# A convolution and expert kernel of one core: the mask of tiny weights leaves the start, and seven squares, two taps and dummy products move

## The chip, the cores and the metric

The kernel runs on one core of a Trainium2 chip. The metric is the device time of one launch in microseconds (us), the median of several runs. In the profile PE is TensorE, DVE is VectorE, ACT is ScalarE, POOL is GpSimd and SP is SyncE, which here only issues transfers.

## The reference

Two stages follow each other. The first is a causal convolution of seven taps whose weights are a softmax for each position and head. The second is a two-layer network whose activation is a ratio of polynomials.

```python
w = softmax(weight_gen, axis=-1)                   # (4, 4096, 8 heads, 7 taps)
out = np.einsum('bshk,bskhg->bshg', w, x_unf)      # x_unf: 7 shifted copies of x (4, 4096, 192)
x = out.reshape(16384, 192)
h = x @ w_in                                       # w_in (192, 2048), float64
P = a[0] + a[1] * h + a[2] * h2 + a[3] * h3
Q = 1.0 + np.abs(b[0]) * np.abs(h) + np.abs(b[1]) * h2
out = (P / (Q + 1e-06)) @ w_out                    # w_out (2048, 192), float64
```

`weight_gen` and `b` are drawn eight times wider than the rest. The ratio |b0| / (2 sqrt |b1|) is 0.774 for the inputs used here.

## The kernel before

**Tiling.** The 16,384 tokens are cut into 32 chunks of 512, and the 2,048 hidden columns into 8 pairs of 128-column blocks. One chunk with one pair is a slot, so there are 256 slots. Slot n begins a new chunk when n is a multiple of 8.

**A slot.** `m1` (L708) makes the hidden block by 18 products of 512 columns: single-pass products of the high and low parts of data and weights. Then ACT takes |h| (`v1`, L742) and a shifted square (`z1`, L746). DVE forms v(v + rb) from |h| (`d1`, L750), ACT takes its logarithm (`ln`, L759) and an exponential of the negative (`ex`, L762), which is the reciprocal of the denominator. DVE forms the cubic (`w1`, L754) and the ratio (`gg`, L766). `m2` (L721) multiplies by `wo` in two halves of 16 products, `fore` and `aft`. Between the halves stands a `relay`, an empty instruction of SP (L783). The hidden block lies in PSUM in one of three buffers named `h`, so `m1` of slot n + 3 waits for `gg` of slot n. In the start one of the three is taken by `TMP`, the scratch of the weight work.

**Weights.** `w_in` and `w_out` are float64. They are loaded in 14 units: A0 to A3 and B0, B1 for `w_in`, W0 to W7 for `w_out`. `unit` turns each into float32 by hand: ACT reads the low words (`ua2`, L401) and takes the size of the high words (`ua1`, L397), DVE does four steps (`ub1` L406, `ub2` L411, `ub3` L416, `ub4` L421). The step `ub4` multiplies by (size >= TINY), so that a weight below 2^-126 becomes zero. For A and B units the value is then split in a high part (`uh`, ACT, L449) and a low part (`uw`, DVE, L452). Slot n waits for unit W of number n, for A of number n // 2 and for B of number n // 4. Four buffers named `raw` take the loads.

**Chunks.** `chunk` prepares the data: softmax of the tap weights, seven taps, transposition on PE, split by ACT and DVE (L650 to L662), and copies between partitions by transfers (`xd`, `xs`, L672 and L678). All chunks but the first have their taps on POOL (L560, L572, L578). In the first chunk (`early`) DVE does all seven taps (L560) and PE adds them up by products with an identity (`fold`, L596). WARM products with the identity stand before that on PE (L274).

**Order.** All of this is a list of operations with an engine, a duration, a priority key and dependences. `arrange` turns it into one fixed order for each engine by playing it through with the durations written in the list. `OFF`, `KEY`, `PITCH` and `PATIENCE` steer it. An operation with `lock` (here `d1`) is held back in that play while POOL is busy. After the launch's work the kernel reads the flag `slow`, which `judge` (POOL) sets from `a` and `b`; if it is set, a second, plain version runs.

Of the kernel before, what the change touches and what calls it, by code (L numbers as in the profile page):

```python
# [8 lines left out]
FP32 = mybir.dt.float32  # L9
# [35 lines left out]
PITCH = 4.8729  # L45
OFF = {
    "g": 12.72, "ex": 3.33, "ln": 5.25, "v": 13.04, "z": 5.74, "d": 7.0, "w1": 3.82, "m2": 3.16,
    "aft": 4.99, "step": 2.35, "cast": -1.03, "rest": -13.5, "dup": 13.03, "lead": 14.38,
    "w": 45.09, "wW": 10.62, "one": -7.23, "ahead": 52.98, "ul": -53.2,
}  # L50
KEY = {
    "B0": -29.4, "A0": -28.0, "W0": 32.8, "A1": 30.0, "W1": 12.93, "W2": 43.45, "W3": 10.63,
    "B1": 41.25, "A2": 50.17, "W4": 51.8, "W5": 52.8, "A3": 52.8, "W6": 63.24, "W7": 76.41,
# [4 lines left out]
START = 25.2  # L58

# [31 lines left out]
PATIENCE = 0.302  # L91


def arrange(ops, place):
# [48 lines left out]
    while len(order) < len(ops):  # L143
# [34 lines left out]
        if o.land is not None:  # L178
            pipe = max(pipe, o.end + 1.3) + o.land / RATE
            o.land = pipe + 0.4 - s  # L180
# [12 lines left out]

LAP = {"ACT": 0.09, "DVE": 0.08, "POOL": 0.05}
LOCK = 2.59
RATE = 230.0
LOOSE = ("h", "av", "pv", "g", "mag", "rnd", "t1", "w")
# [3 lines left out]
def kernel(  # L201
# [18 lines left out]
    ab = const.tile([P, 6], FP32, name="ab")  # L220
    mg = const.tile([P, 6], FP32, name="mg")
    cf = const.tile([P, 15], FP32, name="cf")
# [9 lines left out]
    tt = const.tile([P, 2], FP32, name="tt")  # L232
    steep = rt[:, 0:1]
    slow = const.tile([P, 1], I32, name="slow")
# [44 lines left out]
    o_mg = op("ACT", 0.2, -90.0, lambda: nc.scalar.activation(  # L279
        out=mg, in_=ab, func=ACTF.Abs), [o_ab])  # L280
# [25 lines left out]
    o_sg = op("POOL", 0.4, -70.0, sg_, [o_mg])  # L306
# [61 lines left out]
    def unit(u):  # L368
# [46 lines left out]
        def ub3():  # L415
            nc.vector.tensor_tensor(t["w"], t["w"], t["rnd"], op=ALU.add)  # L416
# [560 lines left out]
```

## Time and profile before

| what | value |
|---|---|
| median of 3 runs | 1304.03 us (1303.81 to 1304.39) |
| profiled execution | 1304.49 us, span 1302.7 us |
| PE, DVE, ACT, POOL busy | 1266.2, 1178.8, 1135.5, 863.3 us |
| mean granted clock of PE | 0.987 |

The profiled execution's time has 1.8 us around the span, from the first to the last instruction. A granted clock of 1.0 is 2.4 GHz, one of 0.5 is 1.2 GHz. Busy shares are averages over a start and a long even part and have to be read for each.

### The profile page before, as it was taken

The page shows a single profiled execution, that of the slowest core. Times are in us where ns is not written, and L with a number is a line of the kernel's source. Part 1 is how long each engine was busy: PE and PEld are TensorE (multiplying, and loading weights), DVE is VectorE, ACT ScalarE, POOL GpSimd, SP SyncE. Part 2 cuts the span into 40 slices and gives each one's busy share as a digit, 9 for nine tenths or more (in the row PEclk, how much of TensorE's full clock was granted, in tenths as well). Part 3 has the DMA queues.
Part 4 walks back from the last instruction along what each step waited for, and adds up shares of the span by engine and source line. Part 5 has one row for each costly group of instructions (what it writes and reads, how often), then busy time and mean ns, then how long its engine had stood idle before and what let it go on. Part 6 is the DMA issues. An engine that isn't in the chain of part 4 may idle for free.

```text
span 1302.7 us, 30683 instructions
## 1 busy us (share of the span) xinstructions
PE 1266.2 (97%) x13082; PEld 1154.6 (89%) x13082; DVE 1178.8 (90%) x979; ACT 1135.5 (87%) x1162; POOL 863.3 (66%) x578
## 2 busy tenths in 40 slices
PE   7679999999999999999999999999999999999998
PEld 5568989999999999999999999999899999999997
DVE  7989889999999999999999999999999999999884
ACT  3768989889998988989988989898899998898995
POOL 3945797787666688666678766668866667876200
PEclk8789999999999999999999999999999999999999
DMA  7422212222122122223122122212222212222100
GB/s 182 121 76 79 50 62 55 74 79 80 50 76 62 53 80 79 49 79 77 41 74 80 49 76 80 59 55 80 49 80 76 79 41 74 49 75 80 46 13 15
DMA packets 46291, 89.07 MB, mean 68 GB/s; under 512 B 5426, under 2 KB 27976, under 8 KB 46148
## 3 DMA queue, kind: packets, MB, share of 16 engines
q1 hardware_dynamic: 45860, 87.05, 24.3%
q8 instruction: 104, 1.70, 0.6%
q14 instruction: 39, 0.32, 0.1%
q10 hardware_dynamic: 288, 0.00, 0.0%
HBM read 41.40 MB, written 12.58 MB: 41 GB/s over the span
## 4 chain that ended last, share of the span: by engine, by line
PE 88%; DVE 3%; POOL 3%; ACT 2%; SPq 1%; issue 1%; DMA 1%; DVEq 0%; ACTq 0%; POOLq 0%
PE acc L721 49%; PE h L708 38%; PE h L640 1%; POOL pr L560 1%; POOL at L572 1%; SPq L672 1%; DMA x<-in_x_dram 1%; DVE g L766 0%; ACT av L742 0%; PE h L643 0%; SPq L678 0%; DVE av L750 0%; DVE h L411 0%; DVE xm L662 0%; ACT av L759 0%
## 5 line engine op out<-in xcount | busy, mean ns | idle before, releaser
L721 PE MATMUL acc<-wo,g 64*128 64x192 f32 x8192 | 722.1, 324 | 8.5 <-DVE g L766 5.0
L721 PEld LDWEIGHTS acc<-wo,g 64*128 64x128 f32 x8192 | 682.5, 187 | 37.3 <-SPq L783 8.1
L750 DVE SCALAR_TENSOR_TENSOR av<-av,cf 128x1024 f32<-128x1024 f32 x256 | 464.3, 1814 | 57.7 <-ACT av L742 57.5
L560 POOL TENSOR_TENSOR pr<-x,wn 128x768 f32<-128x768 f32 x186 | 364.8, 1961 | 0.1
L766 DVE SCALAR_TENSOR_TENSOR g<-h,ab,av 128x1024 f32<-128x1024 f32 x256 | 327.2, 1278 | 37.2 <-ACT av L762 33.2
L742 ACT ACTIVATE av<-h 128x1024 f32<-128x1024 f32 x256 | 260.2, 1016 | 82.4 <-PE h L708 78.5
L754 DVE SCALAR_TENSOR_TENSOR h<-pv,cf,h 128x1024 f32<-128x1024 f32 x256 | 326.7, 1276 | 0.8 <-ACT pv L746 0.8
L759 ACT ACTIVATE av<-av,c 128x1024 f32<-128x1024 f32 x256 | 293.0, 1145 | 37.1 <-DVE av L750 37.1
L572 POOL TENSOR_TENSOR at<-at,pr 128x768 f32<-128x768 f32 x155 | 312.5, 2016 | 12.2
L746 ACT ACTIVATE pv<-h,cf,rt 128x1024 f32<-128x1024 f32 x256 | 306.9, 1199 | 0.0
L762 ACT ACTIVATE av<-av 128x1024 f32<-128x1024 f32 x256 | 270.2, 1056 | 3.3
L708 PE MATMUL h<-xm,wh 64*128 64x512 f32 x1024 | 241.6, 461 | 15.4 <-DVE g L766 13.7
L708 PE MATMUL h<-xs,wh 64*128 64x512 f32 x1024 | 208.7, 394 | 1.7 <-DMA xs<-xm 1.7
L708 PE MATMUL h<-xd,wh 64*128 64x512 f32 x1024 | 206.8, 393 | 0.0
L523 POOL TENSOR_SCALAR mx<-mx,cf 128x32 f32<-128x32 f32 x31 | 9.1, 293 | 207.2 <-DVE mx L520 206.8
L708 PEld LDWEIGHTS h<-xm,wh 64*128 64x128 f32 x1024 | 101.7, 188 | 27.6 <-ACT av L759 7.4
L708 PEld LDWEIGHTS h<-xs,wh 64*128 64x128 f32 x1024 | 101.8, 187 | 21.9 <-DMA xs<-xm 2.9
L708 PEld LDWEIGHTS h<-xd,wh 64*128 64x128 f32 x1024 | 101.1, 187 | 19.2
L708 PE MATMUL h<-xs,wl 64*128 64x512 f32 x512 | 103.9, 392 | 0.0
L708 PE MATMUL h<-xm,wl 64*128 64x512 f32 x512 | 103.6, 394 | 0.0
L708 PE MATMUL h<-xd,wl 64*128 64x512 f32 x512 | 103.4, 392 | 0.0
L578 POOL TENSOR_TENSOR as<-at,pr 128x512 f32<-128x512 f32 (+1 forms) x62 | 86.7, 1401 | 2.4
(90 smaller groups left out, 544.6 us busy)
## 6 DMA issues: line engine op xcount, KB each, us to landing
x<-in_x_dram SPq DMA_DIRECT2D x24, 960.0 KB, 4.7
xs<-xm SPq DMA_DIRECT2D x64, 256.0 KB, 4.0
xd<-xm SPq DMA_DIRECT2D x124, 128.0 KB, 2.4
out_dram<-ob SPq DMA_DIRECT2D x32, 384.0 KB, 4.4
wgt<-in_weight_gen_dram SPq DMA_DIRECT2D x32, 112.0 KB, 2.0
raw<-in_moe_w_in_dram SPq DMA_DIRECT2D x12, 256.0 KB, 4.1
raw<-in_moe_w_out_dram SPq DMA_DIRECT2D x8, 384.0 KB, 3.3
x<-in_x_dram SPq DMA_DIRECT2D x4, 768.0 KB, 4.8
```

The costliest lines, as they stand in the source:

```text
L560: eng.tensor_tensor(dst.rearrange("p q (h g) -> p q h g", g=G), t["x"][:, k:k + Q, :].rearrange("p q (h g) -> p q h g", g=G), t["wn"][:, k ...
L572: eng.tensor_tensor(at, at, term, op=ALU.add)
L578: eng.tensor_tensor(t["as"][:, start:start + Q * (hi - lo)].rearrange("p (q d) -> p q d", q=Q), at[:, :, lo:hi], term[:, :, lo:hi], op=ALU ...
L708: nc.tensor.matmul(h[:, f, :], w[half, b_, i, :], v[half, part, 0:N], start=k == 0, stop=k == 8, skip_group_check=True)
L721: done.append(nc.tensor.matmul(acc[:, bank, q_ * D:(q_ + 1) * D], g[half, f, seat(q) * P:(seat(q) + 1) * P], wo[half, 2 * i + f, :], start ...
L742: nc.scalar.activation(out=t["v"], in_=flat(t["h"]), func=ACTF.Abs)
L746: nc.scalar.activation(out=t["z"], in_=flat(t["h"]), func=ACTF.Square, scale=steep, bias=shift)
L750: nc.vector.scalar_tensor_tensor(out=t["v"], in0=t["v"], scalar=rb, in1=t["v"], op0=ALU.add, op1=ALU.mult)
L754: nc.vector.scalar_tensor_tensor(out=flat(t["h"]), in0=t["z"], scalar=lift, in1=flat(t["h"]), op0=ALU.add, op1=ALU.mult)
L759: nc.scalar.activation(out=t["v"], in_=t["v"], func=ACTF.Ln, bias=c0)
L762: nc.scalar.activation(out=t["v"], in_=t["v"], func=ACTF.Exp, scale=-1.0)
L766: nc.vector.scalar_tensor_tensor(out=flat(t["g"]), in0=flat(t["h"]), scalar=a0, in1=t["v"], op0=ALU.add, op1=ALU.mult)
```

## The change

The mask leaves the start: `ua1` and `ub4` are taken out of the 14 units. In their place `verify` loads each unit again, one per chunk from slot 40 on (slots 40, 48, ... 144), takes its size on ACT and on DVE finds the largest size below TINY. At slot 152 the 14 results are joined and put into `slow`; if a tiny weight was found, the plain version runs, which now makes its own masked weights. `judge` also asks that |b0| / (2 sqrt |b1|) is at most 2.

In slots 0 to 6 `d1` of DVE becomes `q1` of ACT: the square of v + rb/2, with the constant put into the bias of the logarithm.

In the first chunk the last two taps (k = 5 and 6) and their sum go to POOL, so that DVE has five taps and PE six folds. The load of `x` of that chunk no longer waits for the small fill of its first row by POOL, and so comes before the first weight load on SP. The copies `xs` of that chunk are issued by ACT.

`a` and `b` are loaded into one partition and spread by one product with a row of ones, where two transfers spread them before.

`fill` puts dummy products with the identity into PE's order wherever the play leaves PE more than 0.9 us without work before 75 us. WARM goes from 30 to 24. All keys and offsets have new values.

```diff
-PITCH = 4.8729
+PITCH = 4.8708
...
+CHECKED = 40
+SQUARED = 7
...
-PATIENCE = 0.302
+PATIENCE = 0.242
...
+def fill(order, filler):
+    done, last = [], None
+    for o in order:
+        if o.eng == "PE":
+            if last is not None and o.start < FILLED and o.start - last > 0.9:
+                done.append(Op("PE", 0.0, 0.0, filler(o.start - last - 0.3)))
+            last = o.end
+        done.append(o)
+    return done
+
+
+FILLED = 75.0
...
-        nc.scalar.dma_start(out=ab[:, 0:4], in_=a.partition_broadcast(P))
-        nc.scalar.dma_start(out=ab[:, 4:6], in_=b.partition_broadcast(P))
-
-    o_ab = op("ACT", 0.9, -300.0, load_ab, land=4.0)
+        nc.scalar.dma_start(out=six[:, 0:4], in_=a.rearrange("(o n) -> o n", o=1))
+        nc.scalar.dma_start(out=six[:, 4:6], in_=b.rearrange("(o n) -> o n", o=1))
+
+    def spread():
+        T["spare"] = tiled(("acc", "warm"), [P, 2, N])
+        nc.tensor.matmul(T["spare"][:, 1, 0:6], one, six, start=True, stop=True)
+
+    o_one = op("DVE", 0.1, -400.0, lambda: nc.vector.memset(one, 1.0))
+    o_ab = op("ACT", 0.9, -300.0, load_ab, land=1.0)
+    o_six = op("PE", 0.2, -300.0, spread, [o_ab, o_one], takes=[("acc", "warm")])
+    o_ab = op("ACT", 0.2, -89.0, lambda: nc.scalar.copy(out=ab, in_=T["spare"][:, 1, 0:6]), [o_six],
+              uses=[("acc", "warm")])
...
-        tile_w = tiled(("acc", "warm"), [P, 2, N])
         for k in range(WARM):
-            nc.tensor.matmul(tile_w[:, 0, 0:P], ident, ident, start=True, stop=True)
-
-    if WARM:
-        op("PE", 0.2 * WARM, -9.0, warm, [o_id], takes=[("acc", "warm")])
+            nc.tensor.matmul(T["spare"][:, 0, N - P:N], ident, ident, start=True, stop=True)
...
+    op("PE", 0.16 * WARM, -9.0, warm, [o_id, o_six], uses=[("acc", "warm")])
...
+        g.tensor_scalar(half_rb, rb, 0.5, None, op0=ALU.mult)
+        g.tensor_tensor(floor_, half_rb, half_rb, op=ALU.mult)
+        g.tensor_scalar(floor_, floor_, -1.0, 1.0 + 1e-6, op0=ALU.mult, op1=ALU.add)
...
-        def ua1():
-            t["mag"] = tiled(("mag", u), [P, width])
-            nc.scalar.activation(out=t["mag"], in_=t["hi"].bitcast(FP32), func=ACTF.Abs)
...
-            nc.vector.tensor_tensor(t["w"], t["w"], t["rnd"], op=ALU.add)
-
-        def ub4():
-            w = t["w"]
-            dst = wo_flat[:, j * 2 * D:(j + 1) * 2 * D] if kind == "W" else w.bitcast(FP32)
-            nc.vector.scalar_tensor_tensor(
-                out=dst, in0=t["mag"], scalar=TINY, in1=w.bitcast(FP32), op0=ALU.is_ge,
-                op1=ALU.mult)
+            dst = wo_flat[:, j * 2 * D:(j + 1) * 2 * D].bitcast(I32) if kind == "W" else t["w"]
+            nc.vector.tensor_tensor(dst, t["w"], t["rnd"], op=ALU.add)
...
-        o = op("DVE", 0.69 * cost, base + 2.0, ub4, [o, p1], uses=[w, mag, TMP])
...
+    def verify(k, u):
+        width, t = size_of(u), {}
+        cost = width / U
+        raw, mag, rnd = ((kind, ("again", u)) for kind in ("raw", "mag", "rnd"))
+        at = due(CHECKED + NS * k)
+
+        def load():
+            t["hi"], _ = fetch(u, tiled(raw, [P, 2, N]))
+
+        def size():
+            t["mag"] = tiled(mag, [P, width])
+            nc.scalar.activation(out=t["mag"], in_=t["hi"].bitcast(FP32), func=ACTF.Abs)
+
+        def small():
+            t["bad"] = tiled(rnd, [P, width], I32).bitcast(FP32)
+            nc.vector.scalar_tensor_tensor(
+                out=t["bad"], in0=t["mag"], scalar=TINY, in1=t["mag"], op0=ALU.is_lt, op1=ALU.mult)
+
+        def most():
+            nc.vector.tensor_reduce(out=worst[:, k:k + 1], in_=t["bad"], axis=AXX, op=ALU.max)
+
+        o = op("SP", 0.9, at, load, takes=[raw], land=512.0 * cost, after=at)
+        o = op("ACT", 0.67 * cost, at + OFF["vs"], size, [o], takes=[mag], uses=[raw])
+        o = op("DVE", 0.69 * cost, at + OFF["vs"], small, [o], takes=[rnd], uses=[mag], lock=True)
+        return op("DVE", 0.6 * cost, at + OFF["vs"], most, [o], uses=[rnd])
...
+    o_verified = [verify(k, u) for k, u in enumerate(LOADS)]
+
+    def widest():
+        nc.vector.tensor_reduce(
+            out=worst[:, len(LOADS):], in_=worst[:, 0:len(LOADS)], axis=AXX, op=ALU.max)
+
+    def lay():
+        nc.sync.dma_start(out=row, in_=worst[:, len(LOADS):])
+
+    def top():
+        nc.vector.tensor_reduce(out=worst[0:1, 0:1], in_=row, axis=AXX, op=ALU.max)
...
+            def few():
+                t["few"] = tiled(("wn", c), [P, K, QH])
+                nc.gpsimd.tensor_tensor(
+                    t["few"][:, K - 2:K, :].rearrange("p k n -> p n k"), t["e"][:, :, K - 2:K],
+                    t["mx"].to_broadcast([P, QH, 2]), op=ALU.mult)
...
+            o = op("POOL", 0.3, k0 - 1, few, [o_mx], takes=[("wn", c)], uses=[E, MX])
+            o = op("POOL", 1.49, k0, pair(K - 2), [o, o_lx], takes=[A5], uses=[X, ("wn", c)])
+            o = op("POOL", 1.49, k0, pair(K - 1), [o, o_lz], takes=[A6], uses=[X, ("wn", c)])
+            o_join = op("POOL", 1.83, k0, join, [o], uses=[A5, A6])
...
-            e, dm, da, lk, eng = dve if early and k in DVE_TAPS else pool
+            e, dm, da, lk, eng = dve if early else pool
             tid = AT if k == 0 and not early else ("pr", (c, k))
-            o = op(e, dm, k0, tap(k, eng), [o_lx, o_wn, first], takes=[tid], uses=[X, WN], lock=lk)
+            if early and k == K - 2:
+                continue
+            if early and k == K - 1:
+                o, tid = o_join, A6
...
+                (nc.scalar if early else nc.sync).dma_start(
...
+        def q1():
+            nc.scalar.activation(out=t["v"], in_=t["v"], func=ACTF.Square, bias=half_rb)
...
-            nc.scalar.activation(out=t["v"], in_=t["v"], func=ACTF.Ln, bias=c0)
+            nc.scalar.activation(
+                out=t["v"], in_=t["v"], func=ACTF.Ln, bias=floor_ if n < SQUARED else c0)
...
-        o_d = op("DVE", 1.28, end - OFF["d"], d1, [o_v], uses=[AV], lock=True)
+        if n < SQUARED:
+            o_d = op("ACT", 1.15, end - OFF["sq"], q1, [o_v], uses=[AV])
+        else:
+            o_d = op("DVE", 1.28, end - OFF["d"], d1, [o_v], uses=[AV], lock=True)
...
+    def filler(spare):
+        def run():
+            for k in range(int(spare / 0.17)):
+                nc.tensor.matmul(
+                    T["spare"][:, 0, N - P:N], ident, ident, start=False, stop=True,
+                    skip_group_check=True)
+        return run
+
+    order = fill(arrange(ops, place), filler)
...
-WARM = 30
-DVE_TAPS = (0, 1, 2, 3, 4, 5, 6)
+WARM = 24
```

## Rows read from the trace of the kernel before

**Rows 1.** The page: busy time by engine, and the clock in 40 slices of 32.6 us.

```profile
PE 1266.2 (97%) x13082; PEld 1154.6 (89%) x13082; DVE 1178.8 (90%) x979; ACT 1135.5 (87%) x1162; POOL 863.3 (66%) x578
...
PEclk8789999999999999999999999999999999999999
```

**Rows 2.** Stages: length, busy time (instructions) of PE, PEld, DVE, ACT, POOL, clock, DMA.

```profile
40.00:50.00 10.00, 5.25 (x32) 4.67 (x34) 8.44 (x9) 7.86 (x10) 9.66 (x7) 0.66 0.33 133
...
120.00:140.00 20.00, 20.00 (x220) 18.71 (x218) 19.21 (x13) 18.14 (x18) 18.63 (x10) 1.00 0.15 51
...
600.00:800.00 200.00, 200.00 (x2119) 184.47 (x2116) 185.64 (x146) 181.42 (x185) 138.34 (x87) 1.00 0.24 65
```

**Rows 3.** Stages of the start, same columns.

```profile
10.00:107.50 97.50, 72.34 (x523) 57.43 (x521) 89.62 (x116) 64.86 (x84) 51.38 (x40) 0.82 0.41 111
...
35.60:107.50 71.90, 52.67 (x445) 45.21 (x441) 65.29 (x75) 54.23 (x64) 40.35 (x27) 0.83 0.28 79
```

**Rows 4.** PE's timeline: start, length, instructions [idle before, what ended it].

```profile
44.75 0.79 PE L708 MATMUL h<-xm,wh 64*128 64x512 f32 x2 [6.15 <-DVE g L766]
...
48.73 1.76 PE L721 MATMUL acc<-wo,g 64*128 64x192 f32 x16
...
81.83 0.79 PE L708 MATMUL h<-xm,wh 64*128 64x512 f32 x2 [7.09 <-DVE g L766]
```

**Rows 5.** DVE in L421, then in L750: length, busy (instructions), clock, DMA.

```profile
0.00:120.00 120.00, 8.59 (x14) 0.86 0.43 116
...
30.00:96.00 66.00, 13.86 (x8) 0.78 0.38 105
```

**Rows 6.** DVE in L560, then ACT in L397, columns as in rows 5.

```profile
0.00:120.00 120.00, 6.41 (x7) 0.86 0.43 116
...
0.00:120.00 120.00, 8.45 (x14) 0.86 0.43 116
```

**Rows 7.** Timeline of the start, SP, ACT and DVE.

```profile
2.44 0.59 SPq L484 DMA_DIRECT2D x<-in_x_dram  x1
...
6.03 0.21 ACT L279 ACTIVATE mg<-ab 128x6 f32<-128x6 f32 x1 [4.01 <-DMA ab<-in_moe_b_dram]
...
9.60 0.68 DVE L406 TENSOR_SCALAR h<-raw 128x512 int32<-128x512 int32 x1
...
12.07 3.56 DVE L560 TENSOR_TENSOR pr<-x,h 128x768 f32<-128x768 f32 x4 [0.21 <-DMA x<-in_x_dram]
...
35.62 1.00 ACT L742 ACTIVATE av<-h 128x1024 f32<-128x1024 f32 x1
```

**Rows 8.** A group of the page: busy, mean ns of one | idle before.

```profile
L746 ACT ACTIVATE pv<-h,cf,rt 128x1024 f32<-128x1024 f32 x256 | 306.9, 1199 | 0.0
```

**Rows 9.** POOL's timeline of the second chunk's taps.

```profile
26.68 1.49 POOL L560 TENSOR_TENSOR at<-x,wn 128x768 f32<-128x768 f32 x1
...
29.70 1.82 POOL L572 TENSOR_TENSOR at<-at,pr 128x768 f32<-128x768 f32 x1
```

**Rows 10.** Stages of 1 us inside the WARM products, columns as in rows 2.

```profile
4.50:5.50 1.00, 1.00 (x7) 1.00 (x7) 0.22 (x1) 0.00 (x0) 0.31 (x1) 1.00 0.57 160
8.50:9.50 1.00, 1.00 (x11) 1.00 (x10) 0.85 (x3) 1.00 (x2) 0.84 (x6) 1.00 1.03 262
```

**Rows 11.** Timeline of the even part, DVE and PE.

```profile
622.05 2.95 DVE L750 SCALAR_TENSOR_TENSOR av<-av,cf 128x1024 f32<-128x1024 f32 x1 [0.56 <-ACT av L742]
624.93 1.27 DVE L766 SCALAR_TENSOR_TENSOR g<-h,ab,av 128x1024 f32<-128x1024 f32 x1
...
627.40 0.53 PE L708 MATMUL h<-xm,wh 64*128 64x512 f32 x2
...
629.61 0.65 PE L721 MATMUL acc<-wo,g 64*128 64x192 f32 x6
```

**Rows 12.** DVE's reductions of a chunk, and the last work of ACT.

```profile
607.79 0.39 DVE L520 TENSOR_REDUCE mx<-e 128x32 f32<-128x224 f32 x1
...
1297.30 0.80 ACT L821 COPY ob<-acc 128x768 f32<-128x768 f32 x1 [10.31 <-PE acc L721]
```

More of the change, by code (lines that the diff above doesn't have):

```diff
@@ L177, in arrange @@
             pool_busy = (s, o.end)
-        if o.land is not None:
-            pipe = max(pipe, o.end + 1.3) + o.land / RATE
+        if o.land is not None and o.land < 0:
+            o.land = o.end - o.land - s
+        elif o.land is not None:
+            pipe = max(pipe, o.end + 1.3)
+            pipe += o.land / rate(pipe)
             o.land = pipe + 0.4 - s
@@ L220 @@
     ab = const.tile([P, 6], FP32, name="ab")
+    six = const.tile([1, 6], FP32, name="six")
+    one = const.tile([1, P], FP32, name="one")
     mg = const.tile([P, 6], FP32, name="mg")
-    cf = const.tile([P, 15], FP32, name="cf")
+    cf = const.tile([P, 17], FP32, name="cf")
+    worst = const.tile([P, len(LOADS) + 1], FP32, name="worst")
+    row = const.tile([1, P], FP32, name="row")
     c0 = const.tile([P, 1], FP32, name="c0")
@@ L305 @@
     inv = tt[:, 1:2]
-    o_sg = op("POOL", 0.4, -70.0, sg_, [o_mg])
+    o_sg = op("POOL", 0.4, -70.0, sg_, [o_mg, o_ab])
     o_r1 = root(1, -70.0, o_sg)
@@ L351, in judge @@
                 g.tensor_tensor(ok, ok, t0, op=ALU.mult)
-        g.tensor_scalar(slow, ok, -1.0, 1.0, op0=ALU.mult, op1=ALU.add)
-    op("POOL", 5.0, 150.0, judge, [o_mg], after=150.0)
+    o_judge = op("POOL", 5.0, 150.0, judge, [o_mg, o_pw], after=150.0)
     ready_w = {}
@@ L436, in unit @@
             return
-        if kind == "A":
-            high, low = (v[:, 0:2, 2 * j:2 * j + 2, :].rearrange("p b n c -> p b (n c)")
-                         for v in (wh, wl))
-        else:
-            high, low = (v[:, 2:3, 4 * j:4 * j + 4, :].rearrange("p b n c -> p b (n c)")
-                         for v in (wh, wl))
+        high, low = place_of(u, wh), place_of(u, wl)
         def words_of():
@@ L456, in unit, with verdict @@
         ready_w[u] = [oh, ol]
+    def verify(k, u):
+        width, t = size_of(u), {}
+        cost = width / U
+        raw, mag, rnd = ((kind, ("again", u)) for kind in ("raw", "mag", "rnd"))
[15 more added lines that the diff above has]
+        return op("DVE", 0.6 * cost, at + OFF["vs"], most, [o], uses=[rnd])
     for u in LOADS:
         unit(u)
+    o_verified = [verify(k, u) for k, u in enumerate(LOADS)]
[6 more added lines that the diff above has]
+        nc.vector.tensor_reduce(out=worst[0:1, 0:1], in_=row, axis=AXX, op=ALU.max)
+    def verdict():
+        g = nc.gpsimd
+        t0, ok = cf[0:1, 13:14], cf[0:1, 14:15]
+        g.tensor_scalar(t0, worst[0:1, 0:1], 0.0, None, op0=ALU.is_le)
+        g.tensor_tensor(ok, ok, t0, op=ALU.mult)
+        g.tensor_scalar(slow, ok, -1.0, 1.0, op0=ALU.mult, op1=ALU.add)
+    at = due(CHECKED + NS * len(LOADS))
+    o = op("DVE", 0.1, at, widest, o_verified)
+    o = op("SP", 0.5, at, lay, [o], land=16.0)
+    o = op("DVE", 0.2, at, top, [o])
+    op("POOL", 0.6, at, verdict, [o, o_judge])
     def chunk(c):
@@ L836, with run @@
         slot(n, made[c][0], made[c][1], made[c][2])
-    order = arrange(ops, place)
+    def filler(spare):
+        def run():
+            for k in range(int(spare / 0.17)):
+                nc.tensor.matmul(
+                    T["spare"][:, 0, N - P:N], ident, ident, start=False, stop=True,
+                    skip_group_check=True)
+        return run
+    order = fill(arrange(ops, place), filler)
     with tc.manual_schedule():
```

133 lines of the change are left out of this document (93 added, 40 removed).

## The prediction, made before the change was run

> **What bounds the kernel now.** First the page. PE is busy for 97% of the span, so the kernel looks bound by PE from end to end; the line of the clock already shows two slices at 0.8 and 0.7 in the beginning [rows 1]. So the second view is the busy time by stages. From 600 to 800 us PE is busy for all 200.00 us, with DVE at 185.64 and ACT at 181.42: there PE is the bound and nothing on the other engines can gain. From 40 to 50 us it is another kernel: PE is busy for 5.25 of 10 us and its clock is 0.66. By 120 us PE is full [rows 2]. From 10 to 107.5 us, where `gg` of slot 9 ends, DVE works 89.62 of 97.50 us, idle for 8.1%; ACT works 64.86 [rows 3]. PE's timeline says the same: its idle times of 6.15 and 7.09 us end by a `gg` of DVE, which frees a block `h` [rows 4]. So the start is bound by DVE, and from there PE sets the pace to the end, with only the last copy and store behind it: ACT's copy starts at 1297.30 us [rows 12]. What the start gains, the end gains, unless the even part loses it again.
>
> All sums go against the profiled execution, 1304.49 us. The median of the runs is 1304.03, so 0.46 comes off at the end. 2.6 us (0.2%) is about what a measurement of this kernel can tell from no change.
>
> **The mask leaves the start.** The 14 steps `ub4` of DVE cost 8.59 us [rows 5], the 14 `ua1` of ACT 8.45 us [rows 6]. Both go. On DVE they stand among work of the bound, so I count them in full.
>
> **Squares on ACT.** Slots 0 to 6 lose `d1`. The eight runs to 96 us took 13.86 us [rows 5]; the eighth, slot 7's, ran at the undisturbed 1.28 us, so the seven took 12.58. ACT gains seven squares. It has no such row; the nearest are the square from PSUM, 1.20 us [rows 8], and the size in 1.00 us [rows 7]. I take 1.20, together 8.4 us (7.0 at the least).
>
> **Taps.** Seven taps of DVE took 6.41 us [rows 6], two are 1.83. POOL gets one small product, two taps of 1.49 and an addition of 1.82 us [rows 9], some 5.4 us with the small one at 0.6 as a guess between nothing and a tap. They run beside DVE's five taps of 4.6 us, so the last fold waits about 1 us for POOL at worst; if POOL shares badly it is more, bounded by the stretch of `d1` beside POOL, 2.95 for 1.28 us [rows 11]. The taps of DVE read their weights from PSUM, and such instructions of DVE kept their time beside POOL (`gg` 1.27 [rows 11]). The Trainium skill (GPSIMD Engine Reference, § Engine selection) advises against POOL for two-input work, as about 2 times slower. Rows here give 1.49 against 0.92 us, a factor of 1.6; by the page's factor the two taps would be about 0.7 us longer, an estimate which my sum does without.
>
> **The earlier beginning.** DVE's first tap waits until 12.07 us for `x`, issued at 2.44 behind the 0.5 MB of unit B0 [rows 7]. Now `x` goes out in B0's place, about 1.2 us earlier, and those 0.5 MB at 262 GB/s [rows 10] are 2.0 us less in front of it: 8.9 us. The softmax must be ready by then. It hung on `b`, which reached ACT at 6.03 us [rows 7], and the first unit step came right behind it at 9.60. Two small transfers to one partition and one product of PE replace it; no row prices them, and I put their gain between nothing and 2.5 us. Taken together I start the taps at 8.5 us, between 8.0 and 9.7.
>
> **Dummies and the clock.** The 18 products of slot 2 took from 44.75 to 48.73, 3.98 us, at the 1.2 GHz level after 6.15 us of idle PE [rows 4]; in the even part they take 2.21 us, from 627.40 to 629.61 [rows 11]. Dummies can save 1.8 us for each such block. A dummy is two instructions: 11 of them in 1 us when fast, 7 when slow [rows 10], so 0.18 or 0.29 us each against the 0.17 with which the gaps are filled. Fast they fit into a gap less 0.3 us almost exactly; slow they overrun. I count one block, 1.8 us, on the way to slot 0 and nothing later. The Trainium skill (TensorE: Matmul & The Clock Gate, § Why this matters for your kernels) asks to keep PE busy because idleness brings the lower clock; the trace agrees, with 0.66 around the idle 6.15 us. By that rule alone the later blocks would gain too, which is the first rival below.
>
> **The checks.** In each of 14 chunks come one or two loads, a size on ACT (0.6 us as `ua1`) and two instructions on DVE. `small` is like `ub4`, 0.61 us, but reads both inputs from SBUF like `d1`, so beside POOL it may stretch by 2.95/1.28 to 1.4. `most` is a reduction; 224 elements took 0.39 us [rows 12], so 512 take between 0.39 and 0.89. Per check DVE gives 1.0 to 2.3 us. What covers it: DVE idles for 14.36 of 200 us [rows 2], some 2.7 us in a chunk (8 slots of 50 instructions of PE and 6 for the transposition, at 2119 in 200 us, make 38 us), and `gg` at 624.93 ends 1.2 us before the product at 627.40 that needs its block `h` [rows 11]. So most of it hides; if the cover is gone, a check costs PE up to 2.3 us. I take 0.2 us each, 2.8 in all, near nothing because a chunk's own reductions and splitting pass today without idle PE. SP issues up to two loads, at 0.59 us each [rows 7], which a `relay` may have to wait for; `m1` lies between the halves and covers 2.2 us. The join at slot 152 is one small round and costs nothing.
>
> **The sum.** DVE: 89.62 - 8.59 - 12.58 - 1.83 = 66.6 us, from 8.5 us on: 75.1, and with today's idle share 66.6/0.919, ending at 81.0. ACT: its first `v1` was at 35.62 us, 23.55 behind the first tap [rows 7]. After 8.5 us it comes 23.55 - 1.83 (taps) - 1.2 (two `ub4`) - 1.8 (clock) later, at 27.2. From there to 107.5 us ACT worked 54.23 us [rows 3]; less seven `ua1` (4.2) and plus 8.4 it is 58.4, ending at 85.6 without idle and, with DVE's idle share as that of an engine that bounds, at 27.2 + 63.5 = 90.7. ACT comes later than DVE, so it sets slot 9: 107.5 - 90.7 = 16.8 us of gain. With 2.8 lost to the checks: 1304.49 - 16.8 + 2.8 - 0.46 = **1290.0 us**.
>
> **Rivals.**
>
> *DVE stays the only bound.* If ACT's work fits in between and the clock stays high, slot 9 ends at 81.0: a gain of 26.5, 1280.3 us. For it: ACT's work lies within one slot's dependences and needs no gaps. Against it: its 58.4 us after 27.2 leave no room. 18%.
>
> *DVE and ACT wait for each other.* Today ACT idles for 17.67 of 71.90 us [rows 3]. If it keeps that 24.6%, slot 9 ends at 27.2 + 77.5 = 104.7 and the gain of 2.8 is what the checks cost: 1304 us. With two blocks `h` and a chain of five ACT steps this can be. Against it: much of that idling is waiting for a DVE that now has 23 us less. 12%, with what lies between.
>
> *Dummies delay real products.* If the gaps are as wide as 6.15 and 7.09 us and the clock is low when they are filled, 34 and 39 dummies of 0.29 us overrun them by 3.7 and 4.2 us: 1290.0 + 7.9 = 1297.9 us. Against it: dense dummies should bring the clock up. 10%.
>
> *The checks break the even part*, the other side. If DVE has no room where they stand (the block `h` has 1.2 us there), each delays PE. From 1.2 us per check on (16.8/14) the gain is gone; at the full 2.3 us it is 32 us, 1304.03 - 16.8 + 32.2 = 1319.4 us. For it: the DVE is at 93% there. 8%.
>
> The forecast has 52%, with a range of its own from 1284 to 1296. The whole range reaches to the first and near the second rival, 1280 to 1300; it also holds the ends of the start (8.0 to 9.7) and the squares at 7.0. Slower: 6% from the checks. Same: 8%, the second rival's end and a part of the fourth. Faster: 86%.
>
> **What would show it.** Right: `gg` of slot 9 ends near 91 us; ACT is the fuller engine from 30 to 85; no `d1` before slot 7; the first tap at 8 to 9 us; PE full from some 95 us on and idle for less than 3 us more between 200 and 800. Wrong: idle PE before `m1` in the chunks with checks, DVE idle beside ACT idle in the start, real products waiting behind dummies, or a flag that sends the launch to the plain version, which would cost a second run of everything; the ratio of 0.774 and weights far above 2^-126 speak against that.

## The result, and the profile after

| | before | after |
|---|---|---|
| median | 1303.92 us (1303.15 to 1304.39, 4 runs) | 1320.95 us (1317.75 to 1322.71, 4 runs) |
| profiled execution, its span | 1304.49 us, 1302.7 | 1317.75 us, 1315.8 |

The change makes the kernel slower: ratio 1.0128, 95% interval 1.0108 to 1.0149. The forecast was 1290.0 us with a range to 1300. The profiled execution was the shortest of the four, 3.2 us under their median.

PE's busy line and the clock on the page of the changed kernel, then its stages (columns as in [rows 2]):

```profile
PE 1291.8 (98%) x13340; PEld 1171.0 (89%) x13340; DVE 1163.8 (88%) x987; ACT 1139.7 (87%) x1170; POOL 871.8 (66%) x591
...
PEclk9999999999999999999999999999999999999999
```

```profile
40.00:50.00 10.00, 6.98 (x41) 5.46 (x42) 3.67 (x5) 4.40 (x6) 9.77 (x7) 0.83 0.65 153
...
600.00:800.00 200.00, 199.38 (x2092) 181.29 (x2090) 190.66 (x158) 180.45 (x184) 141.96 (x91) 1.00 0.25 74
44.76:109.63 64.87, 62.82 (x587) 56.07 (x585) 46.84 (x55) 58.07 (x64) 35.35 (x27) 0.98 0.22 62
```

PE has more busy time and a better clock, and none of that is a gain. From 40 to 50 us DVE, which was busy for 8.44 of 10 us there [rows 2], has 3.67 us of work: it waits for something. From 600 to 800 us PE does 2092 instructions where it did 2119. So there are two losses, one in the start and one in the even part. The timeline of the start, all engines:

```profile
2.94 0.56 PE L297 MATMUL acc<-six,one 1*128 1x6 f32 x2 [2.94 <-DMA six<-in_moe_b_dram]
3.43 7.08 PE L309 MATMUL acc<-ident 128*128 128x128 f32 x48
...
10.55 0.18 ACT L313 ACTIVATE mg<-acc 128x6 f32<-128x6 f32 x1 [8.53 <-PE acc L309]
...
14.31 0.40 DVE L619 TENSOR_TENSOR h<-e,mx 128x224 f32<-128x224 f32 x1
...
16.53 0.16 DVE L326 RECIPROCAL tt<-rt 128x1 f32<-128x1 f32 x1 [1.82 <-ACT rt L322]
...
17.32 3.56 DVE L645 TENSOR_TENSOR pr<-x,h 128x768 f32<-128x768 f32 x4
...
31.93 1.18 SPq L416 DMA_DIRECT2D raw<-in_moe_w_in_dram  x2
32.49 1.56 ACTq L796 DMA_DIRECT2D xs<-xm  x2
33.17 0.58 SPq L566 DMA_DIRECT2D x<-in_x_dram  x1
...
44.76 1.02 ACT L860 ACTIVATE av<-h 128x1024 f32<-128x1024 f32 x1 [9.17 <-PE h L826]
...
48.05 10.31 PE L966 MATMUL acc<-ident 128*128 128x128 f32 x90
...
108.35 1.28 DVE L888 SCALAR_TENSOR_TENSOR g<-h,ab,av 128x1024 f32<-128x1024 f32 x1
```

Four of these rows answer to [rows 7]. The product that spreads `a` and `b` ends at about 3.5 us, but ACT reads its result only at 10.55 us, after the 24 warm-up products (48 records): they write the same PSUM tile, and the wait named in the row is for them. Before, ACT had the same numbers at 6.03 us. The first tap follows at 17.32 instead of 12.07 us, the first |h| at 44.76 instead of 35.62. On the way to the tap there is one more wait: DVE has the weights of the softmax at 14.71 us (L619), but four small steps of the denominator's second root stand ahead of the taps in its order, and the first of them (L326) waits 1.82 us for ACT. In the kernel before they came after the taps, at 22.67 us. The chain of waits has the second cause of the late |h|, the copies `xs` (here the second of the two):

```profile
33.21 10.27 DMA xs<-xm
43.52 4.60 PE h L826 x21
```

From the first |h| on the changed kernel is quicker: `gg` of slot 9 ends at 109.63, 2.1 us behind the kernel before, where |h| was 9.1 us behind. Then it loses again. A step from the first transposition of one chunk to that of the next took 38.4 us before (608.00 to 646.37, for one), and takes 38.7 to 38.9 us from the 11th chunk on, and 39.4 to 40.0 at six of its 20 borders (before, six of the same 20 took 38.7 to 39.0). What PE waits for between 200 and 1250 us, first after (us in total, times, longest), then before:

```profile
PEld acc L839 <- SPq L905: 13.1, 20, 1.6
PE acc L839 <- SPq L905: 5.1, 6, 1.2
```

```profile
PEld acc L721 <- SPq L783: 3.7, 6, 0.8
PE acc L721 <- SPq L783: 1.0, 3, 0.4
```

L905 is the `relay`, the empty instruction of SP between the halves of `m2`. One border between chunks, after:

```profile
1117.68 0.66 PE L758 MATMUL h<-ident,as 128*128 128x128 f32 x4
...
1118.43 1.14 ACT L880 ACTIVATE av<-av,c 128x1024 f32<-128x1024 f32 x1
1119.47 0.79 ACT L771 CAST xm<-h 128x768 fp32r<-128x768 f32 x1
1120.15 0.81 ACT L946 COPY ob<-acc 128x768 f32<-128x768 f32 x1
...
1119.22 1.21 DVE L875 SCALAR_TENSOR_TENSOR h<-pv,cf,h 128x1024 f32<-128x1024 f32 x1
1120.34 0.94 DVE L780 TENSOR_TENSOR xm<-h,xm 128x768 fp32r<-128x768 f32 x1
...
1120.99 0.34 SPq L949 DMA_DIRECT2D out_dram<-ob  x1
1121.44 2.57 SPq L790 DMA_DIRECT2D xd<-xm  x4
1124.12 2.40 SPq L796 DMA_DIRECT2D xs<-xm  x2
...
1126.63 2.87 PE L839 MATMUL acc<-wo,g 64*128 64x192 f32 x32 [1.09 <-SPq L905]
```

SP works in order: the copies `xd` and `xs` end at 1126.52, the relay behind them comes then, and PE has waited 1.09 us. Two things stand ahead of the copies that did not before: the store of the output (L949), which waits for ACT's copy `ob`, and a late split, with `ln` (L880) ahead of its first half (L771) and `w1` (L875) ahead of its second (L780). From the transposition to `xd` it is 3.76 us; before it was 2.73 (1108.17 to 1110.90), with the split ahead of `ln` (L759) and the store (L824) behind the copies. The same border before:

```profile
1108.17 0.66 PE L640 MATMUL h<-ident,as 128*128 128x128 f32 x4
...
1109.08 0.80 ACT L653 CAST xm<-h 128x768 fp32r<-128x768 f32 x1
...
1109.78 1.15 ACT L759 ACTIVATE av<-av,c 128x1024 f32<-128x1024 f32 x1
...
1110.90 2.56 SPq L672 DMA_DIRECT2D xd<-xm  x4
...
1113.57 2.41 SPq L678 DMA_DIRECT2D xs<-xm  x2
...
1116.16 0.45 SPq L824 DMA_DIRECT2D out_dram<-ob  x1
```

### The profile page after: what moved, and what is told of

Read it like the earlier page. It is cut to its first block, busy times and chain, and to the rows that moved or that the text cites. A ratio compares the mean times of both kernels' runs of the same rounds, so it can differ in the third digit from the quotient of the medians.

```text
span 1315.8 us, 31250 instructions
## 1 busy us (share of the span) xinstructions
PE 1291.8 (98%) x13340; PEld 1171.0 (89%) x13340; DVE 1163.8 (88%) x987; ACT 1139.7 (87%) x1170; POOL 871.8 (66%) x591
## 3 DMA queue, kind: packets, MB, share of 16 engines
HBM read 47.69 MB, written 12.58 MB: 46 GB/s over the span
## 4 chain that ended last, share of the span: by engine, by line
PE 91%; ACT 2%; DVE 2%; SPq 2%; issue 1%; DMA 1%; POOL 0%; ACTq 0%; DVEq 0%
PE acc L839 49%; PE h L826 39%; PE acc L966 1%; PE h L758 1%; SPq L790 1%; DMA xs<-xm 1%; SPq L796 1%; PE acc L309 1%; ACT av L860 1%; PE h L761 0%; DVE g L888 0%; ACT ob L946 0%; ACT av L880 0%; DVE pr L645 0%; ACT av L884 0%
## 5 line engine op out<-in xcount | busy, mean ns | idle before, releaser
L868 DVE SCALAR_TENSOR_TENSOR av<-av,cf 128x1024 f32<-128x1024 f32 x249 | 445.3, 1788 | 56.3 <-ACT av L860 55.3
L645 POOL TENSOR_TENSOR pr<-x,wn 128x768 f32<-128x768 f32 x186 | 347.8, 1870 | 0.0
L657 POOL TENSOR_TENSOR at<-at,pr 128x768 f32<-128x768 f32 x155 | 332.6, 2146 | 12.2
L875 DVE SCALAR_TENSOR_TENSOR h<-pv,cf,h 128x1024 f32<-128x1024 f32 x256 | 325.3, 1271 | 6.4 <-ACT pv L864 6.3
L880 ACT ACTIVATE av<-av,c 128x1024 f32<-128x1024 f32 x249 | 284.9, 1144 | 25.3 <-DVE av L868 24.6
L826 PE MATMUL h<-xm,wh 64*128 64x512 f32 x1024 | 238.3, 457 | 1.0 <-DVE g L888 1.0
L826 PEld LDWEIGHTS h<-xm,wh 64*128 64x128 f32 x1024 | 99.6, 186 | 12.3 <-PE acc L839 1.0
```

Source lines behind the costliest of these rows:

```text
L645: eng.tensor_tensor(dst.rearrange("p q (h g) -> p q h g", g=G), t["x"][:, k:k + Q, :].rearrange("p q (h g) -> p q h g", g=G), t["wn"][:, k ...
L657: eng.tensor_tensor(at, at, term, op=ALU.add)
L826: nc.tensor.matmul(h[:, f, :], w[half, b_, i, :], v[half, part, 0:N], start=k == 0, stop=k == 8, skip_group_check=True)
L868: nc.vector.scalar_tensor_tensor(out=t["v"], in0=t["v"], scalar=rb, in1=t["v"], op0=ALU.add, op1=ALU.mult)
L875: nc.vector.scalar_tensor_tensor(out=flat(t["h"]), in0=t["z"], scalar=lift, in1=flat(t["h"]), op0=ALU.add, op1=ALU.mult)
L880: nc.scalar.activation(out=t["v"], in_=t["v"], func=ACTF.Ln, bias=floor_ if n < SQUARED else c0)
```

## The experiments

**1 to 4: one suspect each.** The kernel before beside them had a median of 1303.1 us.

```diff
# 1, spread first                                        # 2, xs by SP
+    for o in (o_mg, o_ab):                              -  (nc.scalar if early else nc.sync).dma_start(
+        order.remove(o)                                 +  nc.sync.dma_start(
+        order.insert(order.index(o_six) + 1, o)
# 3, no dummies: order = arrange(ops, place)             # 4, the functions of verify and of the join do nothing
```

> The changed kernel with one edit: ACT's two reads of the spread a and b stand ahead of the warm-up products in the program; nothing else moves. Theory A (the reads wait for the warm-up since both use one PSUM tile, and this delays the start): the reads come near 4 us where they came at 10.55, the first tap of DVE near 12 us where it came at 17.3, the median falls by 3 to 6 us from about 1320.5 to 1315-1317. Theory B (the first products are held by the landing of xs anyway): the first tap comes earlier, but the first |h| stays near 44.8 us and the median falls by less than 1.5 us.

> The changed kernel with one edit: the two copies xs of the first chunk are issued by SP as before, at the same place of the order. Theory A (a copy issued by ACT lands late, 10.3 us, where SP's took 4): xs lands some 6 us earlier and the median falls by 3 to 5 us. Theory B (the landing is late because weight loads stand ahead of it in the transfer engines, whoever issues): landing and median stay within 1.5 us, or grow, as SP's queue has its loads in front.

> The changed kernel without the dummy products of the gaps; the order is otherwise the same. Theory A (the dummies overrun the gaps and hold real products, 2.5 us before slot 2 and 1.4 us before slot 6): the median falls by 1 to 4 us although the clock drops to 1.2 GHz in places. Theory B (the clock they keep up is worth more): the median grows by 2 to 5 us.

> The changed kernel with the instructions of the 14 checks and of their join left out (the flag then rests on a and b alone); the order of all else is the same. Theory A (the even part is slower because of SP's queue at the chunk's border, not because of the checks): the steps between the transpositions of later chunks stay 0.3 us longer than before, also where no check stood, and the median falls by less than 3 us. Theory B (the fourth rival of the prediction, checks hold PE): the median falls by 10 us or more and the later chunks have 38.4 us again.

Measured: 1316.41 us (ratio 1.0098, 1.0081 to 1.0115), 1314.19 (1.0080, 1.0063 to 1.0097), 1319.93 (1.0125, 1.0108 to 1.0142) and 1319.08 (1.0114, 1.0096 to 1.0132). The spread ahead of the warm-up brings the first tap from 17.32 to 10.31 us, but the first |h| only to 43.62: now the fourth tap waits 5.31 us for the folds, which stand behind a row of dummy products, and `xs` are late as before. `xs` by SP brings |h| to 42.96, with the tap at 18.32. Without the dummies, or without the checks, the time stays within the spread of the changed kernel's own runs (1317.75 to 1322.71); with the checks gone the later steps are 0.28 to 0.37 us too long all the same. So the start has several gates in a row, and the checks are not what slows the even part.

**5 to 8: the starts together, the store, the old constants.** Beside them before took 1303.4 us. `stores` lists the stores of the chunks, `made[c][1][2]` is the copies of chunk c.

```diff
# 5: the store behind the copies and the relay on SP; 6: 1 + 2 + 5; 7: 6 without dummies
+    copies = [made[c][1][2] for c in range(1, NCH)]
+    for o in stores:
+        at = order.index(o)
+        later = [k for k in range(at, len(order)) if order[k].eng == "SP"][:2]
+        if len(later) > 1 and order[later[1]] in copies:
+            k = next(k for k in range(later[1] + 1, len(order)) if order[k].eng == "SP")
+            order.insert(k + 1, o)
+            order.pop(at)
# 8: PITCH, OFF, KEY and PATIENCE of before
```

> The order of SP alone is changed: the store of a finished chunk, which waits for ACT's copy of the output, goes behind the two copies (xd, xs) and the relay that follow it, instead of ahead of them. Theory A: in the changed kernel the store holds the copies back, the copies hold back the relay behind them, and PE waits for the relay (13.1 us in 20 waits in its profile); then the steps from chunk to chunk come back from 38.7 to 38.5 us, the waits for the relay fall below 7 us, and the time falls by 5 to 10 us, to 1311 to 1316. Theory B: the even part is slower because DVE's and ACT's new order leaves gg later, and the relay only shows it; then the time stays within 3 us of 1320.95, and PE waits elsewhere as long.

> Three orders put right together: ACT reads the spread a and b before the warm-up products, SP issues the copies xs of the first chunk, and the store goes behind the copies of the next chunk. Theory A: the late start has two causes that hide each other (the late softmax, 5.3 us at the first tap, and the late landing of xs), so together they give more than the 4 and 6 us that each gave alone: the first |h| comes at 33 to 36 us, gg of slot 9 ends near 98, and with the store the time is 1296 to 1303, faster than before. Theory B: the start is bound by something behind them (DVE's order with the denominator's root step ahead of the taps, or the splitting); then the first |h| stays above 40 us and the time is 1306 to 1314.

> The three orders put right as in the run before it, and no dummy products either. If the dummies gain what the prediction counted for them (1.8 us for one slow block) or more, this is 2 to 6 us slower than the three alone, with PE's clock below 1.0 from 35 to 60 us. If they delay the products behind them (58.30 against 55.5 us for slot 2), it is 2 to 4 us faster. Alone they made 1 us of difference, within the spread.

> All edits of the change, but the four steering constants (pitch, offsets, keys, patience) have the values from before, except for the two new ones, the check's offset (as in the change) and the offset of the square on ACT (that of the d1 that it replaces). Theory A: the even part is slower by some 10 us because of the order that the new values give (the store of a chunk ahead of the copies, the relay behind them); then the steps from chunk to chunk are 38.4 to 38.5 us as before and PE waits less than 8 us for the relay between 200 and 1250 us, whatever the start does. Theory B: the operations of the change themselves make it slower (the later loads, the checks' tiles); then the steps stay at 38.7. The start I expect to be late in any case: ACT still issues xs and still waits for the warm-up products; 1308 to 1325 in all.

Measured: the store late 1317.56 us (1.0102, 1.0082 to 1.0121), the three 1308.22 (1.0036, 1.0021 to 1.0050), without dummies 1306.13 (1.0022, 1.0012 to 1.0031), the old constants 1310.45 (1.0047, 1.0030 to 1.0063). The store alone missed its theory: the waits for the relay stay (12.7 and 5.7 us). With the old constants they are 3.1 and 1.0 us and the steps 38.44 and 38.49 us, so it is the order that the new constants give, and not the new work, that slows the even part. That run also has the copies `xs` by ACT, and the first landed in 3.3 us. Run 6, the three together, brings the first |h| to 38.28 us and the end of `gg` of slot 9 to 101.83, later than theory A had it; without dummies these are 35.07 and 99.52.

**9 to 12: the split ahead of `ln` and `w1`.** Before: 1303.77 us. Run 10 is the old constants with 1 and 2; run 11 is 1, 2, the split and no dummies; run 12 is run 11 with the mask. `lns` and `w1s` list the operations `ln` and `w1`, `made[c][1][:2]` are the two halves of the split.

```diff
# 9: in the 21 chunks from the 11th on where ln (for the cast) or w1 (for the rest) stands directly ahead
+    for c in range(2, NCH):
+        for part, names in zip(made[c][1][:2], (lns, w1s)):
+            at = order.index(part)
+            prior = next(k for k in range(at - 1, 0, -1) if order[k].eng == part.eng)
+            if order[prior] in names:
+                order.insert(at, order.pop(prior))
```

> The changed kernel with one thing moved: in the 21 chunks from the 11th on where ACT's logarithm stands directly ahead of the first half of the split (the cast into xm) and DVE's w1 directly ahead of the second half, the two halves go first. Moving the store left PE's waits for the relay at 18.4 us, so the copies were late for another reason. Theory A: the split ends 0.9 us later after the transposition than before (3.6 against 2.7 us), xd and xs follow it, and the relay behind them on SP comes after PE is ready; then PE's waits for the relay fall from 18.2 us to under 7, the steps of the later chunks from 38.7 to 38.4 to 38.55, and the time by 6 to 10 us, to 1311 to 1315. Theory B: ln and w1, each now 0.8 to 0.9 us later, make gg late and PE waits for it instead; then it is within 3 us of 1320.95.

> The steering constants from before, with the two start orders put right (spread ahead of the warm-up, xs by SP). The constants alone gave 1310.45 us, with steps of 38.44 to 38.49. Theory A (two late waits in the start, added to a steering that hurts the even part): the start gains 8 to 12 us as it did under the new constants, so 1298 to 1303, at or a little below before. Theory B (under the old constants the start is limited by its own order of units): the start gains less than 5 us, 1305 to 1310.

> The change with what the runs so far point to: spread ahead of the warm-up, xs by SP, the split ahead of ln and w1 from the 11th chunk on, no dummy products; the store stays where the change has it. With a store moved as well and without the split it was 1306.13 us, and lost 7.6 us between the transpositions of chunks 11 and 31. Theory A: the split gives 4 to 7.6 of these back: 1298.5 to 1302, faster than before. Theory B: the copies are late for yet another reason: 1304 to 1307.

> The run before it with the mask in the 14 units again (the size on ACT, the masked product on DVE), the checks also kept. By the prediction's term (8.59 us of DVE, counted in full because DVE bounds the start) this costs 8 to 9 us against the run before it. Rival: with the squares on ACT the start waits for ACT and for dependences, so the masked products lie partly in DVE's idle time, and it costs 2 to 5 us.

Measured: 1325.75 us (1.0158, 1.0132 to 1.0183), 1305.80 (1.0016, 1.0006 to 1.0026), 1311.23 (1.0054, 1.0037 to 1.0070) and 1319.53 (1.0127, 1.0110 to 1.0144). The split alone makes it slower, and run 11 misses both its theories. In run 9 the first half of the split now ends early, but `ln` stands between it and ACT's copy `ob`, so the store is later, and the copies behind it too. SP of run 9 at a border whose transposition is at 1126.93:

```profile
1130.40 0.34 SPq L951 DMA_DIRECT2D out_dram<-ob  x1
1130.85 2.56 SPq L790 DMA_DIRECT2D xd<-xm  x4
1133.52 2.48 SPq L796 DMA_DIRECT2D xs<-xm  x2
```

From the transposition to `xd` it is 3.92 us, and the waits for the relay are 18.1 and 7.8 us. In run 5 the store was behind, and `xd` waited for the split; in run 9 the split was early, and `xd` waited for the store. The mask costs 8.3 us (run 12 less run 11); in the two traces `gg` of slot 9 ends 6.4 us later with it (106.96 against 100.52). Under the old constants the repaired start gains 4.7 us, and `gg` of slot 9 ends at 107.96, no earlier than before the change. The dummies are still in that run, and the folds begin at 16.81 us behind a row of them, so it does not tell how much of this the old order causes.

**13 to 16: both gates, and the rest of the start.** Before: 1303.9 us. Run 13 is 5 + 9; run 14 is 1 + 2 + 5 + 9 without dummies; run 15 is run 14 with `d1` on DVE in slots 0 to 6; run 16 is run 14 with this on SP:

```diff
+    at = order.index(made[0][1][2])          # the copies xs of the first chunk
+    prior = next(k for k in range(at - 1, 0, -1) if order[k].eng == "SP")   # the load of a unit
+    order.insert(at, order.pop(prior))
```

> The changed kernel with both moves of the even part: the store behind the copies and the relay, and the split ahead of ln and w1 from the 11th chunk on. In the run with the split alone the split ended early, but the copies then waited for the store, which waits for ACT's copy of the output, and that copy had moved behind ln. Theory A (two gates on one queue, each hidden by the other): the waits for the relay between 200 and 1250 us fall from 18.2 to under 6 us, the steps from the 11th chunk on to 38.4 to 38.6, and the time to 1309 to 1314. Theory B (the copies are late for a third reason): 1317 or more and over 12 us of waits.

> All repairs together: spread ahead of the warm-up, xs by SP, no dummy products, the store behind the copies, the split ahead of ln and w1. Under theory A the lead that the start has at chunk 11 (7.3 us against before) is kept to the end, but for 1 to 2 us: 1297 to 1300, below both kernels. Under theory B 1306 or more, as without the split.

> The run before it with d1 of DVE again in slots 0 to 6, in the places in the order that the change gives to the squares. The prediction took the seven d1 off DVE at 12.58 us and put 8.4 us on ACT, with ACT the later of the two. If DVE is what the start waits for, this costs 8 to 13 us against the run before it; if ACT is, it gains up to 5; if both wait for each other, it is within 3 us.

> All repairs, and on SP the load of the unit that stands directly ahead of the copies xs of the first chunk goes behind them. With that load ahead the copies landed 6.2 us after their issue, against 3.4 us before the change, and PE waited 4.5 us for them. If the landing of xs sets the first |h|, that comes some 2 to 3 us earlier and the time falls by 1.5 to 3 us against the run with all repairs. If the weights or ACT set it, the difference is below 1 us, or the load, now later, costs its slots something.

Measured: 1311.48 us (1.0052, 1.0035 to 1.0069), 1300.05 (0.9970, 0.9959 to 0.9982), 1304.67 (1.0003, 0.9993 to 1.0013) and 1296.21 (0.9941, 0.9924 to 0.9957). Both gates opened, the waits for the relay of run 13 are 3.1 and 0.7 us, its steps 38.55 us, and the same border reads (transposition at 1113.88):

```profile
1116.61 2.56 SPq L790 DMA_DIRECT2D xd<-xm  x4
1119.27 2.24 SPq L796 DMA_DIRECT2D xs<-xm  x2
1121.68 0.47 SPq L951 DMA_DIRECT2D out_dram<-ob  x1
...
1121.63 2.55 PE L839 MATMUL acc<-wo,g 64*128 64x192 f32 x28
```

It is 2.73 us from the transposition to `xd` again, and PE's row has no wait. Two moves that did 3.4 us of good and 4.8 of harm alone do 9.5 us of good together. The first two figures are hardly more than starts differ by: in runs 4, 5, 9 and 13, whose edits touch nothing ahead of the first |h|, it is at 46.74 to 48.93 us, where the changed kernel had 44.76. The stretch from the transposition of chunk 11 to that of chunk 31 leaves the start out: 780.8 us in the changed kernel, 779.5 with the store late, 786.4 with the split early, 772.4 with both, and 771.0 in the kernel before. Run 15 lies between the outcomes expected of it. Runs 14 and 16 beat both kernels. In run 16 the first |h| is at 32.09 us, 3.09 earlier than in run 14, and the time 3.8 us shorter: the landing of `xs` was on the path.

**17 and 18: the dummies and the checks on the fastest kernel.** Before: 1303.5 us.

```diff
# 17: run 16, with                                       # 18: run 16, with
-    order = arrange(ops, place)                         +    for o in ops[first:]:      # all of verify
+    order = fill(arrange(ops, place), filler)           +        o.fn = lambda: None   # and of the join
```

> The fastest kernel so far (all repairs, and the copies xs ahead of the load: 1296.21 us) with the dummy products of the change again. By the prediction's term they save 1.8 us (one slow block): 1294.4. By the rival they delay real products: 2 to 8 us slower, 1298 to 1304, with the folds of the first taps or an m1 behind a row of dummies.

> The same fastest kernel with the checks left out: no second load of the weights, no size, no search for tiny weights, and the flag is set from a and b alone. The order of everything else stays. By the prediction's term (0.2 us for each of 14) it is 2.8 us faster, 1293.4. If the checks lie in idle time altogether, as the unchanged steps of 38.55 us suggest, it is within 1 us.

Measured: 1301.63 us (0.9987, 0.9977 to 0.9996) and 1297.48 (0.9950, 0.9933 to 0.9966; runs from 1294.73 to 1297.56). The checks cost nothing that can be told; the dummies cost 5.4 us. PE of run 17, then two of its stages, then the same stages of run 16:

```profile
10.70 4.85 PE L970 MATMUL acc<-ident 128*128 128x128 f32 x42
15.39 5.33 PE L681 MATMUL h<-pr,ident 128*128 128x384 f32 x16
...
39.54 10.31 PE L970 MATMUL acc<-ident 128*128 128x128 f32 x90
49.79 0.50 PE L826 MATMUL h<-xm,wh 64*128 64x512 f32 x2
```

```profile
10.00:40.00 30.00, 29.66 (x212) 24.58 (x212) 21.80 (x37) 9.43 (x16) 14.80 (x15) 1.00 0.73 196
40.00:60.00 20.00, 19.71 (x189) 18.24 (x187) 12.32 (x15) 17.47 (x20) 14.80 (x13) 1.00 0.38 92
```

```profile
10.00:40.00 30.00, 19.21 (x77) 11.37 (x76) 26.29 (x43) 14.21 (x21) 18.83 (x18) 0.79 0.86 236
40.00:60.00 20.00, 16.50 (x142) 14.59 (x144) 12.54 (x16) 17.68 (x21) 15.36 (x13) 0.80 0.13 33
...
32.09:96.42 64.33, 50.75 (x447) 44.32 (x445) 47.88 (x58) 58.13 (x64) 40.65 (x31) 0.88 0.30 86
```

With dummies the granted clock is at the level of 2.4 GHz in both stages, without them it lies between that and 1.2 GHz. Yet the folds of the first taps begin at 15.39 instead of 11.19 us behind a row of 21 dummies, and `m1` of slot 2 begins at 49.79, 2.5 us after `gg` of slot 0 (46.03 and 1.28 us long) had freed its block.

## Why the prediction was wrong

The forecast for the profiled execution was 1290.5 us, the profiled time 1317.75: 27.3 us apart. They lie in three stretches. Of the first one's 17.6 us, 8.8 lie before the first tap (17.32 against 8.5) and 8.7 behind it.

| stretch | forecast | measured | apart |
|---|---|---|---|
| start to the first \|h\| | 27.2 | 44.76 | +17.6 |
| first \|h\| to the end of `gg` of slot 9 | 63.5 | 64.87 | +1.4 |
| from there to the end | 1199.8 (before 1197.0, and 2.8) | 1208.1 | +8.3 |

**What held.** The middle stretch, on which most of the working went. ACT has 58.07 us of work in it (58.4 forecast) and is fuller than DVE with 46.84; in the fastest kernel the stretch takes 64.33 us. PE is busy for 62.82 us there with the dummies, but for 50.75 without them (run 16), so it does not set the stretch. The terms behind it were right: the seven squares took 8.08 us (8.4), two taps of POOL 2.94 with 1.82 for the sum as forecast, DVE's five taps 4.50 (4.6). Putting the mask back cost 8.3 us in the medians, 6.4 up to slot 9 in the traces (8.59 forecast on DVE). Putting `d1` back cost 4.6 us; by the prediction's own sums DVE would then end at (66.6 + 12.58)/0.919 + 8.5 = 94.7 instead of ACT's 90.7, 4.0 us. The checks hide, as forecast, and cost less than the 2.8 us: `small` took 0.68 and `most` 0.69 us for 512 elements, without the stretch beside POOL that I allowed for. The rival of the checks, the only one of mine on the side where the result came out, gave 1319.4 us, which is near, but falls with runs 4 and 18: its mechanism is not what happened.

**The step that failed first: the taps "between 8.0 and 9.7".** I priced the product that spreads `a` and `b` at a gain between nothing and 2.5 us. I priced the instruction and not its tile. It writes `T["spare"]`, the tile of the WARM products, and ACT's reads of it wait for the products behind it in that tile. It lost 4.5 us at `mg` (6.03 to 10.55) and 5.25 at the first tap. A loss was not among my bounds, though the diff shows both products in one tile. The tile is not all of it: with the reads ahead of the warm-up the first tap comes at 10.18 us (run 16), still beyond my 9.7. There DVE has the softmax weights at 7.57 us, but the steps of the second root stand ahead of the taps and wait 1.82 us for ACT; I had only `x` and `b` in the sum. No run moved the root, so what it costs in the end is open.

**The second: `xs` on ACT, which I did not price at all.** From the issue of `xs` to the first |h| it was 7.1 us (28.54 to 35.62) and is 12.3 (32.49 to 44.76). The queue alone is not to blame, since under the old constants (run 8) the copies from ACT's queue landed in 3.3 us. The copies in run 8, then in the kernel before, with KB each and us from issue to landing (the trace has the landing of the first copy only):

```profile
xs<-xm ACTq DMA_DIRECT2D x2, 256.0 KB, 3.3
```

```profile
xs<-xm SPq DMA_DIRECT2D x2, 256.0 KB, 3.4
```

What differs is what is in flight beside them: 0.5 MB of a unit issued from 0.56 us ahead, and 0.96 MB of the next chunk's `x`, which SP issues 0.68 us behind the first copy, as it no longer has `xs` to issue first. With both beside them PE had the first copy 9.0 us after its issue and the second after 10.3 (3.4 and 3.8 before). On SP behind the unit, with `x` 1.4 us behind, the first landed in 4.6 to 6.7 us, and with the unit moved behind them the kernel gained 3.8 us. The change's own plan lets the copies land 2.6 us after their issue whatever else is in flight (`land=-2.6` in its code). No run left the copies on ACT and moved the unit or `x`, so their shares, and whether two queues side by side matter beside that order, are open. The Trainium skill (DMA: Bandwidth & Descriptors, § Issuing engines are not separate DMA queues) says that transfers share the same DMA engines and interleave whichever engine issues them. These numbers agree: 3.3 us from ACT's queue, 3.4 from SP's.

**The third: SP, of which I said that a `relay` may have to wait for two loads.** I looked at what the new loads do to SP's queue and not at what new constants do to the order on it. The split 0.9 us later and the store in front of the copies use up the 2.2 us that `m1` covers, and PE waits up to 1.6 us. Between the transpositions of chunks 11 and 31 the change loses 9.8 us, and the two moves give 8.4 of them back. The sign that I named was blind to it: PE's idle time between 200 and 800 us rose by 1.8 us only, within the 3 that I allowed, while PE did 59 instructions fewer of 6337. Most of the waiting is PEld's.

**The dummies.** I forecast a gain of 1.8 us, and a rival with 7.9 us of loss because the clock would be low while they run. The clock is high, and they cost 5.4 us. The price was wrong: 45 dummies take 10.31 us, 0.23 each where the gap was filled at 0.17. The kernel before shows the same price, which I misread as 0.18: a count in 1 us takes in the products that reach over its edges [rows 10]. Its WARM products from 8.41 us on, 33 records or 16.5 products in 3.85 us, took 0.23 each; the 13.5 ahead of them, from 2.54 us on, took 0.43 each, where I had 0.29:

```profile
8.41 3.85 PE L274 MATMUL acc<-ident 128*128 128x128 f32 x33
```

45 times 0.06, less the 0.3 us left free, is 2.4 us; 2.5 to 2.8 was measured before `m1` of slot 2. And a row filled by a plan in which the taps come late stands in the way when they come early (4.2 us at the folds). The Trainium skill (TensorE: Matmul & The Clock Gate, § Why this matters for your kernels) asks for a TensorE without idle gaps. The clock agrees, with 1.00 against 0.79 and 0.80. But from the first |h| to slot 9 it is worth 0.7 us here (37.55 to 101.14 in run 17, 63.6 against 64.3 us), while the first |h| came 5.5 us later.

The fastest kernel ends 6.2 us above the forecast: 4.9 before the first |h| (1.7 of them before the first tap), 0.8 in the middle, the rest behind. What stays open is some 0.1 us in each step of the later chunks (38.55 us against 38.36 to 38.45 before), which neither the checks nor the relay explain: PE takes 4.69 us for most slots of all these runs, and 4.65 for some of those before.

## What to carry to other kernels

Price a moved operation by everything that shares its tile and its queue: what must end before its reader may start, what is in flight beside its transfer, and what stands behind it. Where two waits stand one behind the other on an in-order queue, taking away one shows nothing, or a loss; take away both before the theory is dropped. Steering constants that are changed along with the work are an edit of their own, and here they cost 9.3 us between the transpositions of chunks 11 and 31 (780.8 against 771.5 in run 8), nearly as much as the repaired start saves (`gg` of slot 9 ends at 96.42 in run 16, 107.50 before).

## What the runs showed of the hardware that I had not expected

The first of two copies of 256 KB took 3.3 us from issue to landing on ACT's queue (run 8) and 3.4 on SP's (before), and 9.0 us where 0.5 MB and 0.96 MB of loads were in flight beside it (the changed kernel). A product of 128 columns with the identity took 0.23 us with the clock at 2.4 GHz, the WARM products and the dummies alike.
